# One SBUF-to-SBUF copy moved from GpSimd's DMA queue to ScalarE's, and one normalisation from ScalarE to VectorE

## The chip, the cores and the metric

The kernel runs on one core of one Trainium2 chip. A core has TensorE (matrix multiplications into PSUM), VectorE, ScalarE and GpSimd (element-wise work), SyncE (issues transfers) and 16 DMA engines that move data between HBM and SBUF and within SBUF. Each engine works through its own list of instructions in order; semaphores make one wait for another. A transfer can be issued from SyncE, from ScalarE or from GpSimd. The metric is the time of one execution on the device in microseconds (us).

## The reference

The inputs are A_q, A_k, A_v (1 x 2048 x 448), a short filter shift_k (448 x 4), a long filter ssm_k (448 x 2048), a gain ssm_D (448), and an MLP over the sequence (w1 2048 x 1792, w2 1792 x 2048, with biases), all bf16.

```python
h  = x + _A_ref(_layernorm(x), A_k, A_v, ...)      # x = A_q
    k_shift[s] = sum over 4 taps of k[s - t] * shift_k[:, t]
    kv = k_shift * v
    y  = irfft(rfft(kv, 2S) * rfft(ssm_k, 2S))[:S]  # causal convolution of length S, per channel
    out = q * (y + kv * ssm_D)                      # q = _layernorm(x)
h2 = h + _B_ref(_layernorm(h), w1, b1, w2, b2)
    h = _layernorm(x); u = gelu(h^T w1 + b1); y = u w2 + b2   # mixes the 2048 positions, per channel
```

So there is a convolution along the sequence for each of 448 channels, gated by the normalised input, and then an MLP along the same sequence axis.

## The kernel before

**The convolution.** The sequence of 2048 is laid out as 128 partitions times 16 rows (row r of partition q is position 16 q + r), and each row is 448 channels wide. The convolution is done as a transform in two stages by matrix multiplication (`emit_stage1`, `emit_stage2`) for the filter (tag `k1`, `k2`) and for the signal (`u1`, `u2`), a product with complex numbers, and an inverse transform in two stages: `i1` (inside `emit_products_i1`) and `i2` (`emit_i2`). Between the two inverse stages the data have to change partitions: the result of `i1`, in the array TU, is copied by DMA into the array TZ, which `i2` reads.

**The inverse stage i1 and its copies.** `emit_products_i1` runs over eight pairs jj. In each, VectorE forms the products (line 1159), TensorE multiplies (line 1176, h = 0 and 1 for the two halves of a complex number), ScalarE or VectorE moves the PSUM result to TU (`evac`, lines 737 to 741), and two columns j = 2 jj and 2 jj + 1 of TU are copied to TZ (lines 1195 and 1207). The pairs do not run in the order of their numbers; the last pair to run is jj = 7. Its first column (par = 0) is copied in two halves by SyncE, each as soon as its half is evacuated; its second column (par = 1) is copied whole, both halves together, by GpSimd:

```python
k = op(("sp", "pool")[par], lambda e, W, src=src, dst=dst: e.dma_start(dst, src),
```

**Rows 0 and 1.** For these two rows the last pair isn't read from TZ but straight from TU (four more matmuls each, line 1309), so their remaining two matmuls (line 1315) wait only for the copies of the earlier pairs. All other rows wait for the copies of the last pair as well.

**Inverse stage i2 and the norms.** For each of the 16 output rows TensorE makes two matmuls (line 1315), whose weights are tables ET. ET is the transposed table E: TensorE transposes it in parts (line 1106, `ct`), ScalarE copies each part from PSUM (line 737, `128x1024 f16`). For rows 0 to 3 the normalised input XN is prepared ahead by `emit_xn` (steps `xn.1`, `xn.2`, `xn.4`, `xn.5` for rows 0, 1, 2, 3), on ScalarE (line 1276) or on VectorE (line 1278); VectorE then combines PSUM and XN (line 1345). From row 4 on a gate from PSUM comes first (ScalarE line 1325 or VectorE line 1327), then the combination (line 1335). Statistics of the result (VectorE lines 1351 and 1354, or ScalarE line 1363, with small steps on GpSimd) lead to a normalised bf16 row (VectorE line 1394), which is an input of the MLP.

**The MLP.** The first layer accumulates over the 16 rows: seven of the fourteen blocks of 128 units are accumulated while i2 still produces rows (line 1441), the other seven afterwards (line 1451). GELU is on ScalarE (line 1431), the second layer on TensorE (line 1463), the sum with h on VectorE (line 1466).

**What sets the order.** Every operation is recorded with what it reads and writes. The order of each engine's list is written out by hand in `ORDER`, one string for each engine; a token `i1.16:21` is operation 21 of step `i1.16`, and `4-5` stands for operations 4 and 5. `SLOTS` gives the PSUM bank of each buffer. The recorder then places the semaphore waits that the data and the buffers need. Transfers issued by GpSimd take their semaphores from a ring of 8, and a transfer waits until the last one that had its semaphore has landed; transfers issued by SyncE or ScalarE share a ring of 112. Around the change the lists are:

```python
act:  ... i1.16:18 i1.16:9 ct.0:8 xn.4:0 xn.5:0 xn.2:0 ct.1:8 ct.2:8 i2.46:0 ...
dve:  ... q.8:0 xn.1:0 i2.3:0 i2.11:0 i2.4:0 i2.12:0 ...
pool: ... i1.4:20 i1.4:21 i1.16:21 i1.4:19 q.4:4 q.6:4 q.4:5 q.6:5 ...
sp:   ... i1.4:18 i1.16:20 i1.16:19 w1a.1:0 w1a.2:0 ...
```

TensorE's list there is `i1.16:10-17 i1.16:1-8 ct.0:0-7 warm.0:0 i2.1:0-3 ct.1:0-7 i2.9:0-3 i2.2:0-1 i2.10:0-1 ct.2:0-7 i2.45:0-1 i2.17:0-1 ...`, where `i2.1`, `i2.9` are the four matmuls from TU for rows 0 and 1, `i2.2`, `i2.10` their two from TZ, and `i2.45`, `i2.17`, `i2.41`, `i2.20`, `i2.54`, `i2.28`, `i2.32` are rows 7, 2, 6, 3, 8, 4, 5. On VectorE `i2.3` and `i2.11` combine rows 0 and 1, `i2.18` and `i2.21` rows 2 and 3, and `i2.8` is the norm of row 0 for the MLP. The three loads `w1a.1` to `w1a.3` of weights on SyncE wait for all three copies of the last pair.

Of the kernel before, what the change touches and what calls it, by code (L numbers as in the profile page):

```python
# [37 lines left out]
    "act": (  # L38
# [9 lines left out]
    ),  # L48
    "dve": (
# [14 lines left out]
    ),  # L64
    "pool": (
# [13 lines left out]
    ),  # L79
# [118 lines left out]
class _Sched:  # L198
# [50 lines left out]
    def op(self, W, fn, r=(), w=(), br=(), bw=(), n=0, kind=None, est=None, dmab=None, keng=16, rate=None, after=(), safter=(), mode=0):  # L249
        if (self.tag, self.t0) != self.step:  # L250
            self.step = (self.tag, self.t0)
            self.count[self.tag] = self.count.get(self.tag, -1) + 1
        o = _Op()
        o.id = len(self.ops)
        o.engs = W if isinstance(W, tuple) else (W,)
        o.eng = None
        o.fn = fn
        o.is_dma = dmab is not None
        o.nbytes = dmab or 0
        o.keng = keng  # L260
        o.lat = 2000.0 + o.nbytes / (22.0 * keng) if o.is_dma else 0.0
        if o.is_dma:
            o.est = {e: (585.0 if e == "pool" else 700.0 if keng <= 8 else 460.0) for e in o.engs}
        elif est is not None:
            o.est = dict(est) if isinstance(est, dict) else {e: est for e in o.engs}
        else:
            o.est = {e: self.est_of(e, n, kind) for e in o.engs}
        o.ev = None
        o.mode = mode
        o.step = "%s.%d" % (self.tag, self.count[self.tag])  # L270
        o.rate = rate or (208.0 if keng == 8 else 425.0)
        o.tag = self.tag
        o.acq = []
        o.bufs = []
        o.extra = []
        preds = set(after)
        spreds = set(safter)
        for spec in r:
            for c in self._cells(spec):
                preds.update(c.w)  # L280
                c.r.append(o.id)
        for spec in w:
            g = spec[2] if len(spec) > 2 else None
            for c in self._cells(spec):
                rd = [x for x in c.r if x != o.id]
                if g is not None and c.g == g and not rd:
                    preds.update(c.gb)
                    c.w.append(o.id)
                else:
                    base = rd if rd else list(c.w)  # L290
                    preds.update(base)
                    c.w = [o.id]
                    c.r = []
                    c.g = g
                    c.gb = base
        for b in br:
            if len(self.ops) and all(self.ops[x].engs == ("pe",) for x in b.writers):
                preds.add(b.writers[-1])
            else:
                preds.update(b.writers)  # L300
            b.readers.append(o.id)
            o.bufs.append(b)
            b.users.append(o.id)
        for b in bw:
            if not b.writers:
                o.acq.append(b)
            else:
                spreds.add(b.writers[-1])
            b.writers.append(o.id)
            o.bufs.append(b)  # L310
            b.users.append(o.id)
        preds.discard(o.id)
        spreds -= preds
        o.preds = sorted(preds)
        o.spreds = sorted(spreds)
        self.ops.append(o)
        return o.id
# [259 lines left out]
def _build(nc, A_q, A_k, A_v, A_shift_k, A_ssm_k, A_ssm_D, B_w1, B_b1, B_w2, B_b2, out):  # L577
# [54 lines left out]
    with ctx:  # L632
        sch = _Sched(nc, ctx, n_dma_sems=112, small_off=SMALL)
        op = sch.op
# [514 lines left out]
        def emit_products_i1():  # L1149
            for jj in range(R // 2):  # L1150
# [31 lines left out]
                if jj == R // 2 - 1:  # L1182
                    for h in range(2):
                        for par in range(2):
                            j = 2 * jj + par
                            p0 = 64 * (j & 1) + 32 * ((j >> 1) & 1) + (j >> 2)
                            if (h, par) == (0, 1):
                                continue
                            if par:
                                src = TU[0:8 * (R - NZ), j].rearrange("p c d -> p (c d)")  # L1190
                                dst = TZ[p0:p0 + 29:4, NZ:R].rearrange("p r c d -> p r (c d)")
                            else:
                                src = TU[0:8 * (R - NZ), j, h]
                                dst = TZ[p0:p0 + 29:4, NZ:R, h]
                            k = op(("sp", "pool")[par], lambda e, W, src=src, dst=dst: e.dma_start(dst, src),
                                   r=[(o_TU + 2 * j * DB, 2 * DB)] if par else [(o_TU + (2 * j + h) * DB, DB)],
                                   w=[(o_TZ + NZ * 2 * DB, (14 - NZ) * 2 * DB, "zpool"), (o_TZ + 28 * DB, 4 * DB, "zsp")],
                                   dmab=8 * (R - NZ) * DB * (1 + par), keng=8)
                            shuf["zpool"] = k
                            shuf.setdefault("zl", []).append(k)  # L1200
                    continue
# [324 lines left out]
```

## Time and profile before

| | us |
|---|---|
| Three runs | 170.54, 170.13, 170.56 (median 170.54) |
| The profiled execution | 170.53 |
| Its span in the profile | 168.7 |
| TensorE matmuls busy | 159.9 (95% of the span) |
| VectorE, ScalarE, GpSimd busy | 101.8, 90.5, 58.0 |
| Granted TensorE clock | full (1.0) in the whole span |

A line of the timeline gives the start and the length of a group of instructions in us from the start of the span, the engine, the line of the kernel, the operation and its operands, the number of instructions, and in brackets how long the engine was idle before and what ended that. PE is TensorE's matmuls, PEld its weight loads, DVE VectorE, ACT ScalarE, POOL GpSimd; SPq and ACTq are issues of transfers on SyncE and ScalarE. Matmuls are pipelined: a group's length holds the latency of the last one. The chain that ended last is followed back from the last instruction to what released it; "issue" in it is time in which an engine waited for nothing that the profile shows as an instruction, and the landing of a transfer can be such a thing. An answer on DMA gives for each queue its packets, megabytes and share of the 16 engines in the window asked for (q0 GpSimd's, q1 SyncE's, q10 ScalarE's), and for transfers that were issued in it the time from issue to landing, where the trace has it.

### The profile page before, as it was taken

The page shows a single profiled execution, that of the slowest core. Times are in us where ns is not written, and L with a number is a line of the kernel's source. Part 1 is how long each engine was busy: PE and PEld are TensorE (multiplying, and loading weights), DVE is VectorE, ACT ScalarE, POOL GpSimd, SP SyncE. Part 2 cuts the span into 40 slices and gives each one's busy share as a digit, 9 for nine tenths or more (in the row PEclk, how much of TensorE's full clock was granted, in tenths as well). Part 3 has the DMA queues.
Part 4 walks back from the last instruction along what each step waited for, and adds up shares of the span by engine and source line. Part 5 has one row for each costly group of instructions (what it writes and reads, how often), then busy time and mean ns, then how long its engine had stood idle before and what let it go on. Part 6 is the DMA issues. An engine that isn't in the chain of part 4 may idle for free.

```text
span 168.7 us, 3560 instructions
## 1 busy us (share of the span) xinstructions
PE 159.9 (95%) x1416; PEld 92.9 (55%) x1416; DVE 101.8 (60%) x191; ACT 90.5 (54%) x130; POOL 58.0 (34%) x154
## 2 busy tenths in 40 slices
PE   6999999989899999869999999999999999999994
PEld 2786745443333233434554545555577777777783
DVE  7998999999999999989987440000002313132231
ACT  3599858899999999989675803103640000000000
POOL 8346728685820456565777330000000000000000
PEclk9999999999999999999999999999999999999999
DMA  5999898893859766648999999930000111101111
GB/s 173 400 337 380 272 301 314 334 335 123 242 115 307 263 207 185 198 130 267 391 398 401 422 423 421 419 133 0 0 0 12 46 54 54 54 3 56 54 54 54
DMA packets 15532, 35.15 MB, mean 208 GB/s; under 512 B 3780, under 2 KB 9620, under 8 KB 15516
## 3 DMA queue, kind: packets, MB, share of 16 engines
q1 hardware_dynamic: 12396, 28.26, 46.0%
q0 software_dynamic: 2976, 6.58, 12.2%
q8 instruction: 11, 0.18, 0.5%
q10 hardware_dynamic: 144, 0.08, 0.2%
q14 instruction: 5, 0.04, 0.1%
HBM read 22.05 MB, written 1.84 MB: 142 GB/s over the span
## 4 chain that ended last, share of the span: by engine, by line
PE 73%; ACT 12%; DVE 5%; issue 3%; DMA 3%; POOL 2%; DVEq 0%; ACTq 0%
PE ps L1463 25%; PE ps L1441 13%; PE ps L1451 13%; ACT arena L737 7%; PE ps L1315 4%; PE ps L964 3%; ACT arena L1067 3%; PE ps L1092 3%; PE ps L1023 3%; PE ps L1057 3%; DMA arena<-arena 3%; PE ps L1036 3%; PE ps L990 2%; DVE arena L1159 2%; ACT arena L738 2%
## 5 line engine op out<-in xcount | busy, mean ns | idle before, releaser
L1466 DVE SCALAR_TENSOR_TENSOR arena<-ps,arena 128x448 bf16<-128x448 f32 (+2 forms) x17 | 11.1, 656 | 55.8 <-PE ps L1463 55.8
L1463 PE MATMUL ps<-arena 128*128 128x448 bf16 (+2 forms) x238 | 42.7, 342 | 0.0
L1463 PEld LDWEIGHTS ps<-arena 128*128 128x128 bf16 x238 | 33.3, 145 | 9.5
L1441 PE MATMUL ps<-arena 128*128 128x448 bf16 x112 | 23.5, 353 | 0.0
L737 ACT CAST arena<-ps 128x896 bf16<-128x896 f32 (+1 forms) x29 | 23.1, 934 | 0.0
L1067 ACT CAST arena<-ps 128x896 bf16<-128x896 f32 x24 | 20.3, 915 | 4.3 <-PE ps L1057 3.7
L1451 PE MATMUL ps<-arena 128*128 128x448 bf16 x112 | 22.3, 352 | 0.0
L1073 POOL DMA_DIRECT2D arena<-arena x32 | 17.7, 558 | 8.3 <-ACT arena L1067 8.0
L1431 ACT ACTIVATE arena<-ps,arena 128x448 bf16<-128x448 f32 x14 | 8.2, 632 | 19.3 <-PE ps L1451 10.3
L1092 PE MATMUL ps<-arena 128*64 128x448 bf16 x128 | 15.5, 361 | 1.7 <-ACT arena L738 0.7
L1451 PEld LDWEIGHTS ps<-arena 128*128 128x128 bf16 x112 | 11.0, 98 | 10.2
L1441 PEld LDWEIGHTS ps<-arena 128*128 128x128 bf16 x112 | 10.7, 98 | 10.7 <-DVE arena L1394 1.1
L1159 DVE TENSOR_TENSOR arena<-arena 128x1792 bf16<-128x1792 bf16 x16 | 16.5, 1082 | 0.0
L1176 PE MATMUL ps<-arena 64*128 64x448 bf16 x128 | 14.1, 351 | 1.1 <-ACT arena L737 0.5
L1057 PE MATMUL ps<-arena 128*32 128x448 bf16 x256 | 14.6, 355 | 0.4 <-ACT arena L1067 0.3
L1207 POOL DMA_DIRECT2D arena<-arena x16 | 9.3, 585 | 13.9 <-ACT arena L737 12.9
L1092 PEld LDWEIGHTS ps<-arena 128*64 128x64 f16 x128 | 5.3, 108 | 11.0 <-ACT arena L737 3.2
L1176 PEld LDWEIGHTS ps<-arena 64*128 64x128 f16 x128 | 5.2, 94 | 9.8 <-DVE arena L1159 3.1
L1394 DVE TENSOR_SCALAR arena<-arena 128x448 bf16<-128x448 f32 x16 | 7.6, 508 | 4.8 <-POOL arena L1387 4.8
L1057 PEld LDWEIGHTS ps<-arena 128*32 128x32 f16 x256 | 5.3, 95 | 7.6 <-ACT arena L1067 2.6
L1243 DVE BATCH_NORM_STATS2 arena<-arena 128x6 f32<-128x448 bf16 x16 | 9.4, 612 | 0.0
L1005 DVE TENSOR_TENSOR arena<-ps,arena 128x512 bf16<-128x512 f32 (+1 forms) x16 | 9.0, 614 | 0.2
(99 smaller groups left out, 189.0 us busy)
## 6 DMA issues: line engine op xcount, KB each, us to landing
arena<-in_B_w_dram SPq DMA_DIRECT2D x8, 896.0 KB, 10.3
arena<-in_B_w_dram SPq DMA_DIRECT2D x2, 2048.0 KB, 17.3
arena<-arena SPq DMA_DIRECT2D x16, 224.0 KB, 3.8
arena<-arena POOLq DMA_DIRECT2D x32, 112.0 KB, 3.8
arena<-in_B_w_dram SPq DMA_DIRECT2D x2, 1536.0 KB, 18.8
arena<-arena POOLq DMA_DIRECT2D x14, 196.0 KB, 4.0
arena<-in_A_k_dram SPq DMA_DIRECT2D x4, 448.0 KB, 5.5
arena<-in_A_v_dram SPq DMA_DIRECT2D x4, 448.0 KB, 9.0
```

The source lines that it names most:

```text
L737: return e.copy(out=dst(), in_=src())
L1057: op("pe", lambda e, W, b=b, r=r, q=q, x=x, c0=c0: e.matmul(PS[32 * q:32 * q + 32, b.slots[x], 0:D], E[:, 2 * r + x, c0:c0 + 32], src[:, r ...
L1067: return e.copy(out=dst, in_=Ppair(b)) if W == "act" else e.tensor_copy(out=dst, in_=Ppair(b))
L1073: shuf[tag].append(op(q_, lambda e, W, g=g, i=i, a=a, nu=nu, jh=jh: e.dma_start(T[a + i:a + i + 4 * nu - 3:4].rearrange("p (j k) c d -> p ...
L1092: op("pe", lambda e, W, b=bs[h], h=h, j=j, c=c, par=par: e.matmul(PS[64 * par:64 * par + 64, b.slots[c], 0:D], FW[:, 64 * c:64 * c + 64], ...
L1159: op("dve", lambda e, W, m=m, i=i: e.tensor_tensor(out=MR(m.slots[0]).rearrange("p (x y) d -> p x y d", x=2), in0=TU[:, i].unsqueeze(2).br ...
L1176: k = op("pe", lambda e, W, b=bs[h], m=ms[h], par=par, t=t, tab=tab, xy=xy, P=P: e.matmul(Pb(b, par), tab[P, :], MR(m.slots[0])[P, xy, :], ...
L1243: op("dve", lambda e, W, bs=bs, r=r: e.bn_stats(out=bs, in_=XR(r)), r=[(oX(r), DB)], w=[(ob, 24)], n=D, kind="1x")
L1441: op("pe", lambda e, W, r=r, fc=fc, b=bs[fc]: e.matmul(Pb(b), W1A[:, r, 128 * fc:128 * fc + 128], Q[:, r, :], start=(r == 0), stop=(r == R ...
L1451: op("pe", lambda e, W, r=r, fc=fc, b=b: e.matmul(Pb(b), W1B[:, r, 128 * (fc - n0):128 * (fc - n0) + 128], Q[:, r, :], start=(r == 0), sto ...
L1463: op("pe", lambda e, W, r=r, fc=fc, b=b, d0=d0, d1=d1: e.matmul(Pb(b)[:, d0:d1], W2[fc // 7][:, fc % 7, r:S:R], G[:, fc, d0:d1], start=(fc ...
L1466: op("dve", lambda e, W, r=r, b=b, A=A, d0=d0, d1=d1: e.scalar_tensor_tensor(out=XR(r)[:, d0:d1], in0=Pb(b)[:, d0:d1], scalar=bm[:, r:r + ...
```

## The change

The copy of the second column of the last pair (`i1.16:21`) is issued by ScalarE, directly behind ScalarE's evacuation of the half that comes last (`i1.16:9`), and no longer by GpSimd. With it it takes its semaphore from the other ring. The norm of row 1 (`xn.2`) goes from ScalarE, where it was the third of three, to VectorE, behind the norm of row 0 (`xn.1`). Everything else keeps its order. In the file the strings also write `4-5` as two tokens, which names the same operations, and the longer strings move all lines below by two.

```diff
     "act": (
-        ... i1.16:18 i1.16:9 ct.0:8 xn.4:0 xn.5:0 xn.2:0 ct.1:8 ct.2:8 ...
+        ... i1.16:18 i1.16:9 i1.16:21 ct.0:8 xn.4:0 xn.5:0 ct.1:8 ct.2:8 ...
     "dve": (
-        ... q.8:0 xn.1:0 i2.3:0 i2.11:0 ...
+        ... q.8:0 xn.1:0 xn.2:0 i2.3:0 i2.11:0 ...
     "pool": (
-        ... i1.4:20 i1.4:21 i1.16:21 i1.4:19 q.4:4 ...
+        ... i1.4:20 i1.4:21 i1.4:19 q.4:4 ...
...
-                            k = op(("sp", "pool")[par], lambda e, W, src=src, dst=dst: e.dma_start(dst, src),
+                            k = op(("sp", "act")[par], lambda e, W, src=src, dst=dst: e.dma_start(dst, src),
```

52 rows, old and new, of the table ORDER are left out of this document.

## The prediction

> **What bounds the kernel now.** I read the chain that ended last first, then the timeline around the edited lines, then the DMA answers for the transfers in flight there. The chain (start, length, what; all in us) is TensorE's almost from end to end, and around the edit it holds two stretches in which TensorE waited for something that has no compute instruction behind it ("issue"):
>
> ```profile
> 71.99 0.76 PE ps L1309 x4
> 72.74 0.62 issue
> 73.36 0.92 PE ps L1315 x4
> 74.28 0.45 PE ps L1106 x8
> 74.73 0.75 issue
> 75.47 2.81 PE ps L1315 x14
> ...
> 78.47 1.01 PE ps L1441 x5
> ...
> 123.74 42.08 PE ps L1463 x231
> ```
>
> From 75.47 to the end the chain has no further hole, so only time taken out of (or put into) what precedes the first L1441 can move the end. One matmul takes 0.76 / 4 = 0.19. The four L1315 at 73.36 are output rows 0 and 1; the fourteen at 75.47 are rows 7, 2, 6, 3, 8, 4, 5 in this order, two each.
>
> The timeline (start, length, engine, line, idle before it and its releaser) and the landings of two GpSimd transfers, the one issued at 69.08 and the edited one of 70.85, with the span of landings of all L1207 transfers in between:
>
> ```profile
> 69.08 1.15 POOL L1207 DMA_DIRECT2D arena<-arena  x2 [1.41 <-ACT arena L737]
> 69.62 1.62 SPq L1195 DMA_DIRECT2D arena<-arena  x2
> 70.85 0.61 POOL L1195 DMA_DIRECT2D arena<-arena  x1 [0.61 <-ACT arena L737]
> 72.42 2.04 POOL L1254 TENSOR_TENSOR arena<-arena 128x4 f32<-128x4 f32 x2
> 73.33 0.51 PEld L1315 LDWEIGHTS ps<-arena 128*128 128x128 f16 x4 [1.03 <-issue]
> 75.44 2.40 PEld L1315 LDWEIGHTS ps<-arena 128*128 128x128 f16 x14 [0.89 <-issue]
> ```
> ```profile
> arena<-arena POOLq DMA_DIRECT2D x1, 196.0 KB, 4.2
> ```
> ```profile
> DMA to landing us min/median/max: 3.4/3.8/4.3
> ```
> ```profile
> arena<-arena POOLq DMA_DIRECT2D x1, 196.0 KB, 4.5
> ```
>
> 69.08 + 4.2 = 73.28, and TensorE loads the weights of row 0 at 73.33: the first hole ends with that transfer, which the change leaves where it is. 70.85 + 4.5 = 75.35, and row 7 starts at 75.44: the second hole, 0.75 long, ends with the edited transfer. The two SyncE copies of L1195, which row 7 also waits for, are done earlier: their queue moves its last packets before 74.0 and is absent from the answer for 74 to 75.
>
> ```profile
> q1 hardware_dynamic: 18, 0.01, 8.4%
> ```
> ```profile
> q0 software_dynamic: 28, 0.04, 11.0%
> ```
>
> **The change, part by part.** The rows of ScalarE, VectorE and TensorE's weight loads that the sum needs:
>
> ```profile
> 69.65 0.91 ACT L737 CAST arena<-ps 128x896 bf16<-128x896 f32 x1
> 70.45 1.02 ACT L737 COPY arena<-ps 128x1024 f16<-128x1024 f16 x1
> 71.36 2.07 ACT L1276 ACTIVATE arena<-arena 128x448 f32<-128x448 bf16 x3
> 73.32 1.00 ACT L737 COPY arena<-ps 128x1024 f16<-128x1024 f16 x1
> 74.77 1.01 ACT L737 COPY arena<-ps 128x1024 f16<-128x1024 f16 x1 [0.45 <-PE ps L1106]
> 76.05 1.48 ACT L1325 ACTIVATE arena<-ps,arena 128x448 f32<-128x448 f32 x2 [0.27 <-PE ps L1315]
> ```
> ```profile
> 72.70 0.50 DVE L1278 TENSOR_SCALAR arena<-arena 128x448 f32<-128x448 bf16 x1
> 73.94 1.27 DVE L1345 SCALAR_TENSOR_TENSOR arena<-ps,arena 128x448 f32<-128x448 f32 x2 [0.75 <-PE ps L1315]
> ...
> 76.46 0.68 DVE L1345 SCALAR_TENSOR_TENSOR arena<-ps,arena 128x448 f32<-128x448 f32 x1
> 77.06 0.08 DVE L1345 DVE_READ_ACCUMULATOR arena<-ps,arena 128x1 f32 x1
> 77.19 0.68 DVE L1345 SCALAR_TENSOR_TENSOR arena<-ps,arena 128x448 f32<-128x448 f32 x1
> 77.80 0.08 DVE L1345 DVE_READ_ACCUMULATOR arena<-ps,arena 128x1 f32 x1
> 77.80 0.51 DVE L1394 TENSOR_SCALAR arena<-arena 128x448 bf16<-128x448 f32 x1
> ```
> ```profile
> 78.36 0.68 PEld L1441 LDWEIGHTS ps<-arena 128*128 128x128 bf16 x5 [0.33 <-DVE arena L1394]
> ...
> 79.16 0.72 ACT L1325 ACTIVATE arena<-ps,arena 128x448 f32<-128x448 f32 x1
> ...
> 79.93 1.25 PEld L1441 LDWEIGHTS ps<-arena 128*128 128x128 bf16 x8 [0.32 <-ACT arena L1325]
> ```
>
> 1. GpSimd loses one issue of 0.61. The 28 KB transfer behind it and the two statistics pairs move up by about that. Their last result (72.42 + 2.04 = 74.46) is first read by ScalarE at 76.05, 1.6 later: worth nothing.
>
> 2. ScalarE gains one DMA issue and the wait for its own evacuation, which ends at 69.65 + 0.91 = 70.56. The trace has no ScalarE issue of this shape, so it is bounded by the nearest:
>
> ```profile
> 166.43 0.37 ACTq L1471 DMA_DIRECT2D out_dram<-arena  x1
> ```
> ```profile
> L1195 SPq DMA_DIRECT2D arena<-arena x2: 668/670/673, 69.6 to 70.6; - x2
> ```
>
> Below 0.37, above 2 x 0.67 = 1.34, if it has to let the SyncE issue of the same moment (70.57) pass. I take 0.67, SyncE's price for the same kind of rows. Behind it stands the copy of transposed tables (70.45), which moves to 70.61 + 0.67 = 71.28 and ends at 72.30 instead of 71.47. Its PSUM slot is the one that row 1's first four matmuls take: they move from 71.99 to 72.35 and end at 72.35 + 0.76 = 73.11, still 0.22 before row 0 may start at 73.33. So an issue up to 0.67 + 0.22 = 0.89 costs nothing, and each tenth beyond that costs a tenth. The norm taken from ScalarE (2.07 / 3 = 0.69) pays the delay back: the next copy starts at 73.32 + 0.83 - 0.69 = 73.46 and ends at 74.46, before the 74.77 of the one after.
>
> 3. VectorE gains one norm of 0.50 behind the one at 72.70: 73.20 to 73.70. It sits in the 0.75 that VectorE waits for row 0; 0.24 is left. If that cover went, because row 0 came earlier by more than 0.24, the rest would be paid in full.
>
> 4. The transfer leaves at 70.61 instead of 70.85 and no longer through GpSimd. The rows bound its landing from both sides: 1.6 (the 80 KB that ScalarE sends at the end) gives 72.2, 4.5 gives 75.1. I take the 3.8 median of its own kind: 74.4.
>
> ```profile
> out_dram<-arena ACTq DMA_DIRECT2D x1, 80.0 KB, 1.6
> ```
>
> TensorE is free for row 7 at 74.73, so the hole of 0.75 closes. Most of that is lost again, because other waits come next. Row 2 takes the PSUM slot that VectorE frees at 73.94 + 1.27 = 75.21, so it starts at 75.27 (was 75.85). Row 6 takes the slot of the copy that ends at 75.78: 75.83 (was 76.23). Row 3 then starts at 76.20 (was 76.60). From here VectorE rules: it works without a gap from 73.94 to the norm of row 0 that ends at 77.80 + 0.51 = 78.31, except before 77.19, where it waits 0.13 for row 3 (its accumulator read at 77.06 shows that it was ready). That 0.13 is gained, and L1441 starts at 78.23 instead of 78.36. A second short wait goes: at 79.93 TensorE waited for the ScalarE gate that ends at 79.16 + 0.72 = 79.88. The gates start with row 7, now 0.3 earlier, and this one some 0.2. That adds 0.07 at most. So of 0.75, 0.13 + 0.07 = 0.20 arrives at the end.
>
> The sum against the profiled execution: span 168.7 and 1.83 around it, 170.53, which is the median of the runs (170.54) within 0.01. 170.53 - 0.20 = 170.33; 0.05 to 0.1 of that I give back for a landing of row 0's transfer slightly disturbed (third rival). Forecast: 170.4.
>
> The Trainium skill, "DMA: Bandwidth & Descriptors", section "Issuing engines are not separate DMA queues", speaks against the change: transfers from all issuing engines run on the same DMA engines and interleave, so another queue saves only issue time. By it 70.61 + 4.5 = 75.1, an estimate on this trace's 4.5, the hole would shrink by 0.24 and not 0.75. No row here decides it.
>
> **The rivals.** (a) Hidden anyway: the copy lands no sooner than before, because it shares its neighbours' bandwidth (4.5 with others beside it, 3.4 at best). At 75.1 row 3 is 0.24 early, VectorE's 0.13 is still gained: 170.4; at 75.4 nothing is: 170.5.
>
> (b) ScalarE queues behind SyncE. Both are released by the same evacuation and both issue at 70.57 to 70.6. If the issues go one after another, ScalarE's takes 1.34, row 0 starts 1.34 - 0.89 = 0.45 later and VectorE's run with it, less the 0.20: 170.8. Against it: nothing in the trace has both queues busy in full. By the Trainium skill, "Perfetto Trace Analysis", section "DMA Instruction — HWDGE (DVE, Sync)", the descriptor generator is shared and locked for each such DMA, and the lock wait counts in the instruction's time; the trace of before cannot confirm this.
>
> (c) Slower: the new copy disturbs the transfer that row 0 waits for. Now the edited copy stands behind it in GpSimd's own queue; after, it moves beside it from about 72.0 (the SyncE issue of 68.81 has its first packets between 70.0 and 70.5, 1.2 to 1.7 later) to 73. Transfers of this kind land between 3.4 and 4.3, 0.9 apart; an overlap of the last 40% gives 0.36, a whole one 0.9. Every tenth past 73.33 is a tenth on VectorE's run. From 0.20 on it outweighs the gain: 170.7 at 0.36, 171.2 at 0.9.
>
> ```profile
> 68.81 0.68 SPq L1207 DMA_DIRECT2D arena<-arena  x1
> ```
> ```profile
> q1 hardware_dynamic: 29, 0.05, 43.5%
> ```
>
> (The second row is the answer for 70.0 to 70.5; for 69.5 to 70.0 SyncE's queue has none.)
>
> (d) Faster: with one transfer fewer on GpSimd, row 0's lands like its kind (3.8). Then the norm on VectorE becomes the limit: 0.24 more, 170.1; if VectorE can also start its norm earlier, below 170.0.
>
> **Chances and range.** The forecast with (a), 170.2 to 170.5: 0.40. (b) 0.20, (c) 0.25, (d) 0.15. A measurement here tells about 0.3% (0.51) from no change. Faster by more: half of (d) and a sixth of the forecast's own chance, 0.15. Slower by more: 0.6 of (c) and half of (b), should ScalarE's issue be dearer than the rows bound it, 0.25. Within: 0.60. The range leaves out the ends of (c) and (d): 169.9 to 171.1; the forecast's own is 170.2 to 170.6.
>
> **What would show it.** In the profile of after: a ScalarE-queue DMA near 70.6, about 0.67 long (1.3 is rival b); the table copy behind it near 71.3; row 0 still at 73.3 to 73.5 (later is c or b, earlier is d); row 7 near 74.8 with little or no "issue" before it; the norm of row 0 on VectorE ending near 78.2; L1441 starting there, and from it on the same 90 us of TensorE. The prediction is wrong if row 0 moves by more than 0.3 either way, or if TensorE shows a new hole after L1441 began.

## The result and the profile after

The changed kernel takes 171.55 us (median of 12 runs, 170.94 to 172.58) against 170.59 for the kernel before (12 runs, 170.13 to 171.42): a ratio of 1.0057, 95% interval 1.0037 to 1.0078. It is slower, and it lies above the predicted range. Timed a second time beside other kernels (below) the ratio was 1.0039 (1.0022 to 1.0056). All ratios compare fast runs alone; one run of the kernel with the issue behind the table copy (175.46, granted clock 0.98) was slow and is left out.

The chain that ended last, of the changed kernel (start, length, what; lines are two higher than before, so L1311, L1317, L1443 answer to L1309, L1315, L1441):

```profile
71.10 0.91 ACT arena L739
...
72.03 1.50 ACTq L1197
...
73.57 1.02 ACT arena L739
...
74.64 0.93 PE ps L1311 x4
75.57 0.76 PE ps L1317 x4
...
76.59 0.68 DVE arena L1347
...
80.31 1.10 PE ps L1443 x5
```

Before, this stretch belonged to TensorE and to the landing of two transfers. Now it runs through ScalarE: its evacuation, its new DMA issue, which takes **1.50** and not 0.67, the copy of tables behind it, the four matmuls of row 1 that wait for that copy's PSUM slot, then row 0. The 0.62 of "issue" in front of row 0 is gone, because row 0 now starts later than its transfer lands. That transfer is the first of the three that GpSimd issues from 70.53 on. Its issue, from the timeline, and its time to landing, from the answer on DMA for that moment:

```profile
70.53 1.70 POOL L1209 DMA_DIRECT2D arena<-arena  x3 [1.40 <-ACT arena L739]
```
```profile
arena<-arena POOLq DMA_DIRECT2D x1, 196.0 KB, 4.2
```

It lands at 70.53 + 4.2 = 74.73, after the same 4.2 as in the kernel before, and row 0 starts 0.68 later, at 75.41.

The timeline of the changed kernel (start, length, engine, line, operation; in brackets the idle time before and what ended it):

```profile
70.13 0.93 PE L1178 MATMUL ps<-arena 64*128 64x448 bf16 x8 [0.20 <-DVE arena L1161]
72.03 1.50 ACTq L1197 DMA_DIRECT2D arena<-arena  x1
73.57 1.01 ACT L739 COPY arena<-ps 128x1024 f16<-128x1024 f16 x1 [1.57 <-PE ps L1108]
75.41 0.92 PE L1317 MATMUL ps<-arena 128*128 128x448 bf16 x4
75.99 1.28 DVE L1347 SCALAR_TENSOR_TENSOR arena<-ps,arena 128x448 f32<-128x448 f32 x2 [0.92 <-PE ps L1317]
77.25 2.82 PE L1317 MATMUL ps<-arena 128*128 128x448 bf16 x14 [0.47 <-DMA arena<-arena]
79.73 0.51 DVE L1396 TENSOR_SCALAR arena<-arena 128x448 bf16<-128x448 f32 x1
80.30 1.12 PE L1443 MATMUL ps<-arena 128*128 128x448 bf16 x5
```

And the start of the last pair in the kernel before:

```profile
68.67 0.93 PE L1176 MATMUL ps<-arena 64*128 64x448 bf16 x8 [0.20 <-DVE arena L1159]
```

The profiled execution of the changed kernel is the longest of its twelve (172.58; span 170.8 against 168.7, 2.1 more). It has to be taken apart before it is read. The matmuls of the last pair start at 70.13 instead of 68.67: 1.46 of the 2.1 was there before anything the edit touches. So I count every time from the start of that pair (the "mark"):

| from the mark | before | after | difference |
|---|---|---|---|
| table copy starts | 70.45 - 68.67 = 1.78 | 73.57 - 70.13 = 3.44 | 1.66 |
| row 0 starts | 73.36 - 68.67 = 4.69 | 75.41 - 70.13 = 5.28 | 0.59 |
| VectorE combines row 0 | 73.94 - 68.67 = 5.27 | 75.99 - 70.13 = 5.86 | 0.59 |
| row 7 starts | 75.47 - 68.67 = 6.80 | 77.25 - 70.13 = 7.12 | 0.32 |
| first matmuls of the MLP | 78.36 - 68.67 = 9.69 | 80.30 - 70.13 = 10.17 | 0.48 |

The span's remaining part behind that is 168.7 - 78.36 = 90.34 before and 170.8 - 80.30 = 90.50 after, 0.16 more. The **stage** (mark to first matmul of the MLP) is thus 0.48 longer. The accounts close: row 0 is 0.59 late, VectorE's run from row 0 to the norm is 79.73 - 75.99 = 3.74 instead of 77.80 - 73.94 = 3.86, 0.12 shorter, and 0.59 - 0.12 = 0.47.

### The profile page after: what moved, and what is told of

Same layout as the page of the kernel before. It is cut to its first block, busy times and chain, and to the rows that moved or that the text cites. A ratio compares the mean times of both kernels' runs of the same rounds, so it can differ in the third digit from the quotient of the medians.

```text
span 170.8 us, 3560 instructions
## 1 busy us (share of the span) xinstructions
PE 160.3 (94%) x1416; PEld 92.3 (54%) x1416; DVE 102.2 (60%) x192; ACT 90.1 (53%) x129; POOL 57.9 (34%) x153
## 4 chain that ended last, share of the span: by engine, by line
PE 62%; ACT 16%; DMA 9%; DVE 6%; issue 2%; SPq 1%; ACTq 1%; POOL 0%; DVEq 0%
PE ps L1465 25%; PE ps L1443 13%; PE ps L1453 12%; ACT arena L739 7%; ACT arena L1069 5%; DMA arena<-in_A_ssm_k_dram 5%; DMA arena<-arena 4%; ACT arena L740 3%; PE ps L1059 3%; DVE arena L1161 2%; PE ps L1094 2%; PE ps L1317 2%; DVE arena L742 1%; PE ps L1038 1%; DVE arena L1347 1%
## 5 line engine op out<-in xcount | busy, mean ns | idle before, releaser
L1443 PE MATMUL ps<-arena 128*128 128x448 bf16 x112 | 23.5, 353 | 0.0
L1443 PEld LDWEIGHTS ps<-arena 128*128 128x128 bf16 x112 | 10.7, 98 | 10.8 <-DVE arena L1396 0.9
L739 ACT COPY arena<-ps 128x1024 f16<-128x1024 f16 (+1 forms) x7 | 6.9, 1013 | 5.2 <-PE ps L966 3.2
```

Of the source, the lines that this page charges most:

```text
L739: return e.copy(out=dst(), in_=src())
L1443: op("pe", lambda e, W, r=r, fc=fc, b=bs[fc]: e.matmul(Pb(b), W1A[:, r, 128 * fc:128 * fc + 128], Q[:, r, :], start=(r == 0), stop=(r == R ...
```

## The experiments

Two questions: does ScalarE's dear issue explain the lost 0.48 (and not a disturbed transfer), and why is it dear? The short diffs are against the changed kernel, unless something else is said; in them `...` leaves out unchanged tokens. Line numbers shift by up to ten between kernels. The table has all runs. Times are from each kernel's mark and of one profiled execution each; the ratio is to the kernel before, timed beside it.

| kernel | ScalarE issue | table copy | row 0 | row 7 | stage | ratio (95%) |
|---|---|---|---|---|---|---|
| before | none | 1.78 | 4.69 | 6.80 | 9.69 | 1 |
| changed | 1.50 | 3.44 | 5.28 | 7.12 | 10.17 | 1.0057 (1.0037 to 1.0078) |
| changed, again | 1.50 | 3.45 | 5.28 | 6.50 | 10.17 | 1.0039 (1.0022 to 1.0056) |
| copy only | 1.50 | 3.45 | 5.28 | 7.12 | 10.43 | 1.0077 (1.0056 to 1.0098) |
| norm only | none | 1.78 | 4.68 | 6.78 | 9.67 | 0.9999 (0.9977 to 1.0022) |
| behind the table copy | 1.50 | 1.77 | 4.32 | 6.30 | 9.21 | 0.9987 (0.9956 to 1.0017) |
| behind the table copy, again | 1.50 | 1.77 | 4.70 | 6.59 | 9.59 | 1.0020 (0.9998 to 1.0042) |
| from SyncE | none | 1.77 | 4.44 | 6.70 | 9.60 | 1.0005 (0.9984 to 1.0026) |
| SyncE's half by GpSimd | 1.27 | 3.21 | 5.05 | 7.07 | 9.95 | 1.0025 (1.0000 to 1.0050) |
| pad of 1.19 | none | 2.87 | 4.68 | 6.39 | 9.57 | 1.0016 (1.0000 to 1.0033) |
| pad of 1.56 | none | 3.24 | 5.05 | 6.86 | 9.94 | 1.0013 (0.9991 to 1.0036) |
| two early copies | 0.73 | 2.69 | 4.75 | 7.07 | 9.96 | one execution, 171.93 |
| two early copies, again | 0.74 | 2.69 | 4.58 | 6.88 | 9.76 | 1.0105 (1.0068 to 1.0142) |
| early load | 1.50 | 3.45 | 5.29 | 6.72 | 10.18 | 1.0031 (1.0010 to 1.0051) |

**The two parts alone.** The copy moved, the norm of row 1 left on ScalarE:

```diff
-act: ... i1.16:9 i1.16:21 ct.0:8 xn.4:0 xn.5:0 ct.1:8 ...
+act: ... i1.16:9 i1.16:21 ct.0:8 xn.4:0 xn.5:0 xn.2:0 ct.1:8 ...
-dve: ... xn.1:0 xn.2:0 i2.3:0 ...
+dve: ... xn.1:0 i2.3:0 ...
```

> The copy issued by ScalarE as in the changed kernel, the norm of row 1 left on ScalarE. ScalarE then has the issue (1.50 us in the changed kernel's profile) and the norm (0.69) on top of each other. Theory 'delayed table copy': row 0 starts as late as in the changed kernel (its first table copy is in the same place), so TensorE's first L1443 stands 10.1 to 10.4 us after the last pair of the first inverse stage (9.7 before, 10.2 changed); the second and third table copies and the gates come 0.7 us later than in the changed kernel and cost 0 to 0.4 more: ratio 1.003 to 1.008. Rival 'norm' (the norm on VectorE is what costs): ratio 1.000 to 1.002.

And the norm moved, the copy left on GpSimd:

```diff
-act: ... i1.16:9 i1.16:21 ct.0:8 ...
+act: ... i1.16:9 ct.0:8 ...
-pool: ... i1.4:20 i1.4:21 i1.4:19 ...
+pool: ... i1.4:20 i1.4:21 i1.16:21 i1.4:19 ...
-k = op(("sp", "act")[par], ...
+k = op(("sp", "pool")[par], ...
```

> The norm of row 1 on VectorE as in the changed kernel, the copy issued by GpSimd as before. Theory 'turns' (ScalarE's issue had to wait for SyncE's, 1.50 us, and the table copy behind it moved rows 0 and 1): the norm sits in VectorE's 0.75 us before row 0, so nothing is lost: ratio to before 0.998 to 1.001. Theory 'own price' (an issue of this copy costs ScalarE 1.5 us by itself): the same. Rival 'norm' (the norm on VectorE delays the combination of row 0): VectorE's combination of row 0 starts 0.2 us or more later after TensorE's row 0, ratio 1.002 to 1.004. Theory 'start' (most of the 0.96 us is lost in the first loads, before the edit, by chance or by layout): ratio anywhere up to 1.005, with the excess already there at the first stage-1 matmuls.

The timeline of the kernel with the norm alone:

```profile
72.89 0.92 DVE L1282 TENSOR_SCALAR arena<-arena 128x448 f32<-128x448 bf16 x2
73.55 0.92 PE L1319 MATMUL ps<-arena 128*128 128x448 bf16 x4 [0.61 <-issue]
74.12 1.28 DVE L1349 SCALAR_TENSOR_TENSOR arena<-ps,arena 128x448 f32<-128x448 f32 x2 [0.31 <-PE ps L1319]
```

Both norms fit into VectorE's wait for row 0, and 0.31 of it is left: the norm costs nothing and gains nothing (0.9999). The copy alone carries the whole loss (1.0077). In the changed kernel the norm even seems to pay something back: without its move the stage is 10.43 instead of 10.17, 0.26 longer (one profile of the copy alone; the intervals of the ratios overlap).

**Where the issue stands, and who issues.** The issue behind the table copy instead of ahead of it; then, in another kernel, the copy sent by SyncE as the third in its row:

```diff
-act: ... i1.16:9 i1.16:21 ct.0:8 xn.4:0 ...
+act: ... i1.16:9 ct.0:8 i1.16:21 xn.4:0 ...
```

> The changed kernel with one step moved: ScalarE issues the copy behind the first table copy, not ahead of it, about 0.9 us later, when SyncE has finished its own issue. 'Turns': the issue takes 0.67 us, rows 0 and 1 start as in the kernel before, ratio 0.998 to 1.001. 'Own price': the issue still takes 1.5 us; rows 0 and 1 are undisturbed, the norms of rows 2 and 3 and the second and third table copies come 0.8 us later, ratio 1.000 to 1.004. 'Start': up to 1.005 whatever the issue takes.

```diff
-act: ... i1.16:9 i1.16:21 ct.0:8 ...
+act: ... i1.16:9 ct.0:8 ...
-sp: ... i1.16:20 i1.16:19 w1a.1:0 ...
+sp: ... i1.16:20 i1.16:19 i1.16:21 w1a.1:0 ...
-k = op(("sp", "act")[par], ...
+k = op(("sp", "sp")[par], ...
```

> The changed kernel with the copy issued by SyncE behind its two halves; ScalarE issues nothing here. 'Turns' and 'own price': ScalarE's table copy is back at its old place, rows 0 and 1 start as before; the copy is issued 0.67 us later than by ScalarE's wish but no later than ScalarE got it, so row 7 starts within 0.4 us of before: ratio 0.998 to 1.002. 'Start': up to 1.005.

The timeline of the kernel with the issue behind the table copy:

```profile
70.29 1.02 ACT L741 COPY arena<-ps 128x1024 f16<-128x1024 f16 x1
70.42 1.50 ACTq L1199 DMA_DIRECT2D arena<-arena  x1
...
72.84 0.92 PE L1319 MATMUL ps<-arena 128*128 128x448 bf16 x4 [0.26 <-issue]
```

The issue is as dear as before, but it started at 70.42, while the copy ahead of it (70.29, 1.02 long) still ran: ScalarE's list issues beside its own running instruction. The table copy is on time again and the loss in the stage is gone. SyncE as issuer loses nothing either. So it is the issue's place on ScalarE's list, not the queue that the copy travels in, that costs time. Neither of the two gains: in the first profile of the issue behind the table copy row 0 was 0.37 early and the stage 0.48 shorter, so I ran that kernel once more.

> The kernel with the copy's issue behind the table copy on ScalarE, once more. If the shorter stage of its first profile (9.21 against 9.69) comes from the edit: stage 9.2 to 9.4 again, row 0 about 4.3 behind the pair's start, GpSimd's transfer for row 0 landing in about 3.9, ratio 0.995 to 0.998. If that was the chance of one execution: stage 9.6 to 9.7, row 0 at 4.7, ratio 0.999 to 1.001.

The timeline, and from the answers on DMA for 68 to 72 us the landing of the GpSimd transfer that row 0 waits for, first in this run and then in the first run of the same kernel:

```profile
73.64 0.92 PE L1319 MATMUL ps<-arena 128*128 128x448 bf16 x4 [0.64 <-issue]
```
```profile
arena<-arena POOLq DMA_DIRECT2D x1, 196.0 KB, 4.2
```
```profile
arena<-arena POOLq DMA_DIRECT2D x1, 196.0 KB, 3.8
```

The same kernel, the same transfer: 4.2 once and 3.8 once, with row 0 at 4.70 and 4.32. The early row 0 was the chance of one execution; the ratio, 1.0020, came out 0.001 above what I expected for that. Over all profiles here this transfer lands after 3.8 to 4.2, whether GpSimd still sends the edited copy (4.2 in the kernel before, 3.8 in the kernel below with a pad of 1.19) or not (4.2 and 4.1 in the changed kernel).

**Is ScalarE's time the whole loss?** Activations of no use in the issue's place, the copy sent by GpSimd as before, the norm on VectorE. First two of 448 columns:

```diff
-act: ... i1.16:9 i1.16:21 ct.0:8 ...
+act: ... i1.16:9 pad.0:0 pad.0:1 ct.0:8 ...
-pool: ... i1.4:21 i1.4:19 ...
+pool: ... i1.4:21 i1.16:21 i1.4:19 ...
-k = op(("sp", "act")[par], ...
+k = op(("sp", "pool")[par], ...
+    for i in range(2):
+        op("act", lambda e, W: e.activation(out=JK, in_=XR(8), func=ACT.Copy), ...
```

> The copy is issued by GpSimd as before, the norm of row 1 is on VectorE; in the place of the issue ScalarE does two added activations of 448 columns, about 0.75 us each, whose result nobody uses. Theory 'delayed table copy': it is ScalarE's 1.5 us ahead of the table copy that cost the time, whatever they are spent on; the table copy ends 1.5 us later, row 0 starts 0.5 to 0.6 us later, the first L1443 stands 10.1 to 10.3 us after the last pair of the first inverse stage: ratio 1.002 to 1.005. Rival 'transfer' (the loss comes from the copy landing on another queue): 9.6 to 9.8 us, ratio 0.998 to 1.001.

The two took 1.19 and not 1.5. The table copy was 2.87 - 1.78 = 1.09 late, and row 0 was not late at all (4.68). That missed what I expected of it, since the pad was too short. It does check the prediction's threshold: there the table copy could move by 71.28 - 70.45 = 0.83, and by 0.22 more, 1.05, before row 0 is late. Then a third activation of 160 columns, the diff against the shorter pad:

```diff
-act: ... pad.0:0 pad.0:1 ct.0:8 ...
+act: ... pad.0:0 pad.0:1 pad.0:2 ct.0:8 ...
-    for i in range(2):
+    for i in range(3):
...
```

> As the run with two padding activations, but the pads on ScalarE now last about 1.5 (two of 448 columns at 0.6 and one of 160 columns): the copy goes out from GpSimd as before, row 1's norm is on VectorE, and no ScalarE issue exists. If ScalarE's time between the evacuation and the table copy is the whole cause of the loss: table copy about 1.5 late, row 0's matmuls about 5.2 behind the start of the last pair (4.69 before, 5.28 changed), first L1441 10.1 to 10.2 behind it (9.69 before, 10.17 changed), ratio 1.002 to 1.006. If something else that the ScalarE issue does is needed (a disturbed transfer, a semaphore), row 0 stays at 4.7 and the stage at 9.7, ratio about 1.000.

The timeline with the longer pad:

```profile
68.79 0.93 PE L1180 MATMUL ps<-arena 64*128 64x448 bf16 x8 [0.20 <-DVE arena L1163]
70.56 1.56 ACT L1265 ACTIVATE arena<-arena 128x448 bf16<-128x448 bf16 x3
72.03 0.99 ACT L741 COPY arena<-ps 128x1024 f16<-128x1024 f16 x1
73.07 0.93 PE L1319 MATMUL ps<-arena 128*128 128x448 bf16 x4 [0.98 <-ACT arena L741]
73.84 0.92 PE L1325 MATMUL ps<-arena 128*128 128x448 bf16 x4
78.73 1.12 PE L1451 MATMUL ps<-arena 128*128 128x448 bf16 x5
```

The table copy is 3.24 - 1.78 = 1.46 late, row 0 5.05 - 4.69 = 0.36, the stage 9.94 - 9.69 = 0.25. In the changed kernel it is 1.66, 0.59 and 0.48: 0.20 more at the table copy gives 0.23 more at row 0 and 0.23 more at the end. The stage came out 0.16 below the least that I expected, by the table copy's 0.20 less delay; the ratio (1.0013) fits 0.25 us but can't be told from none, nor from the shorter pad's (1.0016), so the profile carries this reading. No ScalarE issue is in this kernel, so the delay of ScalarE's list alone gives the stage's loss, one for one. Nothing is left in it for a disturbed transfer, which agrees with the unchanged landing of row 0's transfer (4.2) in the changed kernel.

**Why 1.50?** First the prediction's rival that ScalarE has to let SyncE's issue of the same moment pass: that SyncE issue was given to GpSimd.

```diff
-sp: ... i1.16:20 i1.16:19 w1a.1:0 ...
+sp: ... i1.16:20 w1a.1:0 ...
-pool: ... i1.4:21 i1.4:19 ...
+pool: ... i1.4:21 i1.16:19 i1.4:19 ...
-k = op(("sp", "act")[par], ...
+k = op("act" if par else "sp" if h else "pool", ...
```

> The changed kernel, but the half that SyncE issued at the same moment (released by the same evacuation) is issued by GpSimd; ScalarE's issue stands where the change put it. 'Turns': with SyncE quiet ScalarE's issue takes 0.67 us (0.6 to 0.8), the table copy starts 0.8 us earlier than in the changed kernel and rows 0 and 1 are back: ratio 0.998 to 1.002. 'Own price': still 1.5 us, rows 0 and 1 still 0.6 us late, ratio 1.003 to 1.007.

The row of ScalarE's issue in the timeline of this kernel:

```profile
71.19 1.27 ACTq L1199 DMA_DIRECT2D arena<-arena  x1
```

With SyncE quiet it is still 1.27, between the two lengths that I expected. Company explains 0.23 of the 1.50, no more. So I let ScalarE issue two other SBUF-to-SBUF copies (28 KB each, line 1120) some 20 us earlier, with SyncE's list reordered to make room; the edited copy and SyncE's at the same moment stayed as in the changed kernel.

```diff
-act: ... u2.1:4 u2.9:4 ...
+act: ... u2.1:4 ct0.1:0 ct0.1:1 u2.9:4 ...
-sp: ... u1.15:11 ct0.1:0 ct0.1:1 xload.2:0 xload.3:0 w1a.0:0 ct0.1:2 ct0.1:4 ct0.1:3 ct0.1:5 i1.1:20 ...
+sp: ... u1.15:11 ct0.1:2 ct0.1:4 ct0.1:3 ct0.1:5 xload.2:0 xload.3:0 w1a.0:0 i1.1:20 ...
-                    op("sp", lambda e, W, p0=p0: e.dma_start(
+                    op("act", lambda e, W, p0=p0: e.dma_start(
```

> The changed kernel, with two small copies (28 KB, line 1116 of the kernel before) issued by ScalarE about 20 us earlier, one behind the other, at a time when SyncE has issued nothing for over 4 us; SyncE's loads of that time come later. The edited copy is then ScalarE's third issue. Their lengths tell three theories on the 1.50 us apart. 'Backlog' (ScalarE's issue waits until the shared generator has worked off what SyncE issued in the 2 us before): 0.7 to 0.85 for both early issues, SyncE's own price for them being 0.79, and about 1.5 for the third. 'First use': 1.3 to 1.5, then 0.7 to 0.85, and the third 0.7 to 0.9. 'Own price' (this shape costs ScalarE more than SyncE): 1.3 to 1.5 for all three. The total is not the point: up to 2 us slower from ScalarE's delay.

The timeline of this kernel, all three ScalarE issues and SyncE's two beside the last:

```profile
48.17 1.31 ACTq L1120 DMA_DIRECT2D arena<-arena  x1
49.52 0.70 ACTq L1120 DMA_DIRECT2D arena<-arena  x1
...
70.63 1.62 SPq L1199 DMA_DIRECT2D arena<-arena  x2
71.59 0.73 ACTq L1199 DMA_DIRECT2D arena<-arena  x1
```

The first takes 1.31, the second 0.70, and the edited copy, with SyncE's two issues of 70.63 beside it as in the changed kernel, 0.73. The surcharge, 1.31 - 0.70 = 0.61 for the early copies and 1.50 - 0.73 = 0.77 for the edited one beside SyncE, is on the *first* such issue of the program on ScalarE, whichever copy it is. Timed, and with a second profile:

> The changed kernel with two 28 KB copies of another kind issued by ScalarE some 20 us earlier, once more and timed. If the dearer issue is the cost of the first of its kind on ScalarE: the edited issue takes 0.7 again, the first of the two early ones 1.3; row 0 then is back at 4.7 or a little more behind the pair's start, and the ratio falls below the changed kernel's 1.004 to 1.006: 1.000 to 1.003, unless the early copies cost time of their own elsewhere (their start and SyncE's reordered loads), which a later start of the pair would show. If not: issue 1.5, ratio 1.004 or more.

The timeline of that second profile:

```profile
48.14 1.30 ACTq L1120 DMA_DIRECT2D arena<-arena  x1
49.48 0.71 ACTq L1120 DMA_DIRECT2D arena<-arena  x1
...
69.64 0.93 PE L1180 MATMUL ps<-arena 64*128 64x448 bf16 x8 [0.20 <-DVE arena L1163]
71.55 0.74 ACTq L1199 DMA_DIRECT2D arena<-arena  x1
74.22 0.92 PE L1319 MATMUL ps<-arena 128*128 128x448 bf16 x4
79.40 1.12 PE L1445 MATMUL ps<-arena 128*128 128x448 bf16 x5
```

The three lengths repeat, row 0 is on time (4.58), and the stage is 9.76 instead of 10.17. The ratio missed what I expected (1.0105): the early copies and SyncE's new order cost more than they save, since the pair now starts at 69.64, 0.97 later than before. In this kernel's first profile the stage was 9.96 although row 0 was on time (4.75): there the edited copy landed late, and row 7 began only at 7.07.

Last: is it the first issue of any kind, or the first copy within SBUF? The changed kernel, with one small load from DRAM (4 KB) issued by ScalarE as its very first instruction:

```diff
-act: tables.0:5 ...
+act: loads.14:1 tables.0:5 ...
-sp: ... loads.14:0 loads.14:1 loads.10:0 ...
+sp: ... loads.14:0 loads.10:0 ...
-            op(Dq, lambda e, W: e.dma_start(b2n, B_b2.rearrange("(q r) -> q r", r=R)), ...
+            op("act", lambda e, W: e.dma_start(b2n, B_b2.rearrange("(q r) -> q r", r=R)), ...
```

> The changed kernel, with the last small load at the start (the 4 KB of b2, from DRAM) issued by ScalarE as its first instruction instead of by SyncE, so that ScalarE's first DMA issue of the program is that load. If any first issue on ScalarE takes the extra 0.6: the edited issue falls from 1.50 to about 0.73, the table copy starts about 2.6 behind the last pair's start, row 0 at 4.7, first L1441 at 9.6 to 9.8, ratio 0.999 to 1.002 (the load itself could move the start either way, which the pair's start would show). If only a copy within SBUF pays for its kind: the edited issue stays at 1.50, the stage at 10.1 to 10.2, ratio 1.003 to 1.006.

The timeline of this kernel, at its start and around the edit:

```profile
0.73 0.41 ACTq L913 DMA_DIRECT2D arena<-in_B_b_dram  x1
```
```profile
69.04 0.93 PE L1180 MATMUL ps<-arena 64*128 64x448 bf16 x8 [0.20 <-DVE arena L1163]
70.95 1.50 ACTq L1199 DMA_DIRECT2D arena<-arena  x1
72.49 1.01 ACT L741 COPY arena<-ps 128x1024 f16<-128x1024 f16 x1 [1.57 <-PE ps L1110]
79.22 1.12 PE L1445 MATMUL ps<-arena 128*128 128x448 bf16 x5 [0.17 <-DVE arena L1387]
```

The load takes 0.41, no surcharge, and spares none: the edited copy is back at 1.50. So a first issue of another kind does not take the surcharge away; in these runs it is on the first copy from SBUF to SBUF. One rival is not excluded: a long pause could bring it back. The load stands 70 us ahead of the edited copy, the early copies only 22 us, and no run has a copy within SBUF from ScalarE after a longer pause. What in the chip makes it dear stays open as well.

**The changed kernel again.** It was run as it is, beside other kernels, to see which part of its first profile repeats.

> The changed kernel once more, for a second profile and another interval. In its first profile the span was 2.1 us longer than before, of which 1.45 stood already before the edit (loads at the start that landed later) and 0.5 to 0.6 came at the edit. 'Start by chance': the early 1.45 is not there again (0 to 0.6), the 0.5 to 0.6 at the edit is (first L1443 10.1 to 10.3 us after the last pair), ratio 1.003 to 1.005. 'Start by layout': the early excess is there again with over 1 us, ratio 1.006 to 1.010.

The timeline of the changed kernel in this second profile:

```profile
68.93 0.93 PE L1180 MATMUL ps<-arena 64*128 64x448 bf16 x8 [0.20 <-DVE arena L1163]
70.84 1.50 ACTq L1199 DMA_DIRECT2D arena<-arena  x1
72.38 1.01 ACT L741 COPY arena<-ps 128x1024 f16<-128x1024 f16 x1 [1.57 <-PE ps L1110]
74.21 0.92 PE L1319 MATMUL ps<-arena 128*128 128x448 bf16 x4
75.39 1.48 SPq L1418 DMA_DIRECT2D arena<-in_B_w_dram  x3
75.43 0.54 PE L1319 MATMUL ps<-arena 128*128 128x448 bf16 x2
79.10 1.12 PE L1445 MATMUL ps<-arena 128*128 128x448 bf16 x5 [0.17 <-DVE arena L1387]
```

The issue (1.50), row 0 (5.28) and the stage (79.10 - 68.93 = 10.17) repeat to a hundredth; the late mark doesn't (68.93 against 70.13), so that excess was chance. Here the edited copy landed in time: SyncE's loads of weights, which wait for the last pair's copies, go out at 75.39, and row 7 starts at 75.43 without waiting, 6.50 from the mark, 0.62 earlier than in the first profile. The stage is the same all the same. Row 7's hole did not matter at that size; row 0 and VectorE behind it set the end.

**What stays open.** The stage's 0.48 and the 0.16 behind it are 0.64, or 0.38% of 170.59. That agrees with the second timing (1.0039) and with the kernel with the early load (1.0031), and lies at the lower end of the first (1.0037 to 1.0078). The 0.16 does not come from the late table copy: the part behind the first matmul of the MLP is 168.9 - 78.54 = 90.36 with the norm alone, but 169.0 - 78.53 = 90.47 with the issue behind the table copy, whose stage is not longer. Whether the first timing holds something more was not found. One thing that could add to it, and was not shown: row 0 of the kernel before waits for a transfer that lands after 3.8 to 4.2 in these runs, and the one profile of that kernel has 4.2. Where it lands early, the kernel before gains, while the changed kernel, whose row 0 waits for ScalarE, can't.

## Why the prediction was wrong

**Step 2 failed, at the length of ScalarE's issue.** I took 0.67, SyncE's price for rows of the same kind, with 0.37 and 1.34 as bounds. It was 1.50, above the upper bound. The rest of that step held. Its own working (the table copy may be 0.83 + 0.22 = 1.05 late for nothing) gives 1.66 - 1.05 = 0.61 for row 0 in the changed kernel; 0.59 was measured. With a pad it gives 1.46 - 1.05 = 0.41 against 0.36, and with the shorter pad nothing against nothing. Had the issue's price been known, the sum would have been 170.53 + 0.61 - 0.13 = 171.0; the upper bound came from an engine whose first copy is not dear, the lower from ScalarE's store to DRAM, and no row of the trace showed ScalarE making a copy within SBUF. That corrected sum, 171.0, still lies inside my range; the measured median, 171.55, lies 0.5 above it. So the step explains the sign and the stage, but not the whole distance: 0.16 of the rest stands behind the stage, and what is left above that is the open part of the first timing (the second has 171.37 against 170.76, 0.61 more).

**Step 1** (GpSimd's issue is worth nothing) can't be told apart in these runs. **Step 3** held: the norm sits in VectorE's wait (ratio 0.9999 alone, 0.31 of the wait left against 0.24 predicted). That the norm pays ScalarE's delay back is borne out by one profile of the copy alone: 0.26 of the stage.

**Step 4** was wrong in the landing, and its gain came in another way. I let the copy land 3.8 after its issue. In the first profile row 7, which waited for it, starts 77.25 - 72.03 = 5.22 after the issue; in the second SyncE's loads, which wait for it too, go out 75.39 - 70.84 = 4.55 after it; before, it landed after 4.5. It lands no sooner, counted from the start of its issue, which is rival (a). The Trainium skill's "DMA: Bandwidth & Descriptors", section "Issuing engines are not separate DMA queues", which the prediction weighed against the change, agrees with that: the move bought no transfer time. VectorE's 0.13 wait for row 3, the main gain of the sum, did go (3.86 - 3.74 = 0.12), but by luck as far as my reason goes: I had it from an earlier row 7, and in the first profile row 7 is 0.32 later. VectorE itself began 0.59 later and so found row 3 ready. The longer pad, whose copy GpSimd sends, has the same shortening: from row 0 to the first matmuls of the MLP it takes 9.94 - 5.05 = 4.89, the changed kernel 10.17 - 5.28 = 4.89, the kernel before 9.69 - 4.69 = 5.00. The 0.07 of the late gate is not seen.

**The rivals.** (b) named the place (a long ScalarE issue in front of the table copy, row 0 late) and the sign, but not the cause: waiting for SyncE makes at most 1.50 - 1.27 = 0.23 of it on the first copy and 0.73 - 0.70 = 0.03 on a later one (the 0.70 is of another, smaller copy). The lock on descriptor generation of the Trainium skill's "Perfetto Trace Analysis", section "DMA Instruction — HWDGE (DVE, Sync)", may be that 0.03 to 0.23; the runs do not show it by itself. (c), a disturbed transfer in front of row 0, did not happen: it lands after 4.2, as before, and the pad without any ScalarE issue gives the same loss for the same delay. (d), an earlier landing for row 0, did happen, by chance, in one of two profiles of the same kernel (3.8 and 4.2); the changed kernel's 4.2 and 4.1 do not show it.

**The list of what would show it** did its work: the issue at 1.50 was the line that had to be looked at, and row 0 moved by 0.59, more than the 0.3 that I had set as the limit.

## What to carry to other kernels

An issue on an engine that also computes is paid by what stands behind it in that engine's list. Put it behind the urgent instruction, not ahead of it: here the same issue cost the stage nothing one place further down, where it ran beside the copy. When an engine is given its first transfer of a kind, do not take the price of another engine's transfers, nor that of another kind from the same engine; bound it by more than twice, and ask how long the instruction behind it can wait (here 1.05).

And a transfer that "ends a hole" is worth only what the next wait leaves: with row 7's hole closed (second profile of the changed kernel) the stage did not move, because row 0 and VectorE's run set the end.

## What the runs showed of the hardware

- ScalarE's first SBUF-to-SBUF copy of the program takes 1.27 to 1.31 to issue when SyncE is not issuing at that moment, 1.50 when it is; later ones take 0.70 to 0.74, the last of them 22 us after the one ahead of it. A load from DRAM as ScalarE's first issue takes 0.41 and does not spare the copy its surcharge 70 us later.
- SyncE does not show it in this size. In the kernel before, its first copy of this kind takes 0.63, the others of that line down to 0.54. The row of the timeline, and the answer on that line (duration in ns, least, median and most):

```profile
15.94 0.63 SPq L1073 DMA_DIRECT2D arena<-arena  x1
```
```profile
L1073 SPq DMA_DIRECT2D arena<-arena x16: 536/540/632, 15.9 to 43.9; - x16
```

- ScalarE issues a transfer while its own preceding copy still runs: issue at 70.42 beside a copy from 70.29 to 71.31.
- The same GpSimd transfer of the same kernel landed in 3.8 and in 4.2 in two executions, and the start of the last pair moved between 68.52 and 70.13 over the kernels that change nothing ahead of it. In a kernel of 170 us, one profile does not tell 0.4 us. Counting from a mark just ahead of the edit takes out what differs ahead of it, but not the transfer's own 0.4: the same kernel's stage was 9.21 and 9.59.
